# Linear attention and a gated feed-forward block: the order and the pieces of the first two batches' work

## The chip, the cores and the metric

The kernel runs on one core of a Trainium2 chip. A core has five engines with instruction queues of their own: TensorE (PE; its weight loads are listed as PEld), VectorE (DVE), ScalarE (ACT), GpSimd (POOL) and SyncE (SP). They wait for each other through semaphores. DMA transfers are issued from the queues of SP, ACT and POOL and are moved by 16 DMA engines. The metric is the time of one execution on the device, in microseconds (us); lower is better.

## The reference

For 8 batches with 8 heads each, 576 tokens and a head width of 64, linear attention is computed and then a feed-forward block with a SiLU gate, on 8 x 576 = 4608 tokens of width 512:

```python
q_s = softmax(q, axis=-1)            # over the 64 of a head
k_s = softmax(k, axis=2)             # over the 576 tokens
kv  = einsum('bhsd,bhse->bhde', k_s, v)
x   = einsum('bhsd,bhde->bhse', q_s, kv)      # heads side by side: 4608 x 512
out = (silu(x @ w_gate) * (x @ w_val)) @ w_out   # 512 -> 1536 -> 512
```

Inputs and outputs are float32. The kernel's matmuls take bfloat16 and add up in float32.

## The kernel before

**Layout.** A *group* G is four heads, two groups a batch. A partition of a raw tensor holds nine consecutive tokens (T = 9) of two heads. `load` (L72) reads q, k or v of a group as one transfer of 128 x 2 x 576 float32 values (2304 bytes a row) through SP's queue. [...]

**Attention of a group.** ACT takes the exponential of q and k (`exp_of`, L119). DVE sums exp(q) over each head, inverts the sums (`norm_sum`) and multiplies (`norm_mul`, L146), which gives `qs`. `qs` has to be transposed to `qt`: with nine TensorE transposes into two PSUM banks and two copies (`turn_pe`, `turn_out`), or by a DMA transpose (`turn_dma`, L179). TensorE contracts exp(k) with v over the tokens (`kv_first` for batch 0, `kv_one` for batch 1, `kv_both` later); a column of ones in v, or for batch 0 the matmuls of `key_sum`, gives the sum for k's softmax. The result, divided by that sum, is `kn` (`scale_first`, `scale_one`). `x_mm` multiplies `qt` by `kn`, and `x_out` casts the result into `xt`, the feed-forward block's input, transposed, with 512 features in four slices kk of 128. Slices kk 0 and 1 come from group 0, kk 2 and 3 from group 1.

**Feed-forward.** `m_unit(c0, n, m)` computes 128 of the 1536 hidden features (index m, 12 units a chunk) for n tokens: four gate matmuls (`wg`) and four value matmuls (`wv`) for each part of the tokens, SiLU on ACT (L305), product on DVE (L306) into `hr`. `o_mm(j)` contracts the 12 slices of `hr` with `w_out` for 128 tokens, `o_out` copies and `store` writes. Chunk 0 is batch 0 (576 tokens, in parts of 320 and 256), chunk 1 has 448 tokens, then chunks of 512.

**Order.** The whole program stands under a manual schedule: each engine runs its instructions in the order in which the code calls them, so the lines from L352 on are the schedule. PSUM has eight banks; `bank` (L47) hands them out, and a matmul into a reused bank waits for its last reader.

- *Start, L353 to L383.* SP loads q and k of batch 0, group 0 and then group 1. POOL, after k of group 0 has landed, issues casting transfers to bfloat16: v of group 0, v of group 1 in two pieces (L361), the slices of wg and wv in columns 0 to 255, 256 to 639, 640 to 1023 and 1024 to 1535 (L380), and w_out in four slices. [...]
- *Warm-up, L385 to L391.* `spin(n)` is n matmuls on zeros that nothing reads. Eight at the beginning, six after the first sum of exp(q), six after the first transposes (L426, L427, L435).
- *Batch 0, L428 to L452.* Sums of k, transposes, K^T V, x; then the first unit, which with `by_part` runs the whole first part of the tokens before the second.
- *Loads of batches 1 and 2, L454.* They begin when the second w_out slice has landed.
- *Batch 1, L460 to L493.* Its attention runs between o_mm(0) to o_mm(3), after chunk 0's units. Both its groups are transposed on TensorE. Batches 2 to 7 are computed inside the later chunks, with DMA transposes on SP's queue.

The softmax here doesn't subtract the row's maximum and nothing guards it: scores larger than these inputs give would overflow.

## Time and profile before

| | us |
|---|---|
| median of 12 runs (lowest, highest) | 317.52 (317.2, 318.99) |
| the profiled execution, own time | 317.69 |
| its span, first to last instruction | 315.8 |
| PE busy | 306.7 |
| DVE busy | 162.9 |
| ACT busy | 147.5 |
| first unit of chunk 0 starts | 14.51 |
| o_mm(0) starts, after chunk 0 | 39.17 |
| first unit of chunk 1 starts | 53.21 |

Times inside the span count from its start. In the lists of instructions the columns are start, duration, engine, line, operation, output and inputs, shapes, a count, and in brackets how long the engine had been idle and what ended that. "SPq", "ACTq" and "POOLq" are the queues' own time for issuing transfers. A busy PE is not PE at its peak, since matmuls overlap. In the table of windows the columns are the window, its length, the busy time and the count of instructions of PE, PEld, DVE, ACT and POOL, the granted clock of TensorE, the mean busy share of the DMA engines (over 1.00 when packets overlap) and GB/s.

### The profile page before, as it was taken

How to read it: one execution, taken by the hardware profiler on the slowest of the kernel's cores; microseconds unless marked ns; L12 is line 12 of the kernel's file. 1: busy time of each engine (PE TensorE's matmuls, PEld its weight loads, DVE VectorE, ACT ScalarE, POOL GpSimd, SP SyncE). 2: the span in 40 equal slices, each digit the busy share in tenths (PEclk: the TensorE clock that was granted, in tenths of full speed). 3: DMA queues.
4: the chain of work that ended last, by engine and by line, in shares of the span. 5: the costliest groups of instructions: out<-in, count | busy, mean ns of one | idle time of the engine just before them, and what ended most of it. 6: DMA issues, size and time to landing. Idle time of an engine off the chain costs nothing.

```text
span 315.8 us, 4885 instructions
## 1 busy us (share of the span) xinstructions
PE 306.7 (97%) x1894; PEld 151.9 (48%) x1894; DVE 162.9 (52%) x277; ACT 147.5 (47%) x218; POOL 28.0 (9%) x35
## 2 busy tenths in 40 slices
PE   6799999999999999999999999999999999999994
PEld 2477744554444444444454444544444444444443
DVE  3834486684754566455835492639354333423421
ACT  5843497634673475447454637355743113312300
POOL 2920021101100020002000200020000000000000
PEclk9999999999999999999999999999999999999999
DMA  7999999179246806490639253944310202020124
GB/s 280 184 203 206 301 394 388 54 156 369 53 88 180 336 19 127 107 398 13 141 71 362 84 112 64 323 162 104 66 40 0 66 2 66 0 69 4 31 69 102
DMA packets 39304, 45.75 MB, mean 145 GB/s; under 512 B 16368, under 2 KB 23024, under 8 KB 39280
## 3 DMA queue, kind: packets, MB, share of 16 engines
q1 hardware_dynamic: 32480, 39.99, 42.1%
q0 software_dynamic: 6640, 5.31, 10.9%
q8 instruction: 15, 0.25, 0.3%
q10 hardware_dynamic: 160, 0.13, 0.2%
q14 instruction: 9, 0.07, 0.1%
HBM read 37.75 MB, written 9.44 MB: 149 GB/s over the span
## 4 chain that ended last, share of the span: by engine, by line
PE 90%; DMA 5%; POOL 1%; ACT 1%; DVE 1%; issue 0%; SPq 0%
PE g_ps L298 29%; PE u_ps L298 29%; PE o_ps L322 27%; DMA wv<-in_moe_w_val_dram 3%; PE kv L191 3%; DMA k<-in_k_dram 2%; PE xp L267 1%; PE o_ps L342 1%; POOL wg L99 0%; POOL v L361 0%; DVE qs L152 0%; DVE rs L138 0%; PE tp L166 0%; ACT L124 0%; ACT eq L124 0%
## 5 line engine op out<-in xcount | busy, mean ns | idle before, releaser
L305 ACT ACTIVATE sg<-g_ps 128x512 bf16<-128x512 f32 (+2 forms) x120 | 65.1, 554 | 139.5 <-PE g_ps L298 132.4
L306 DVE TENSOR_TENSOR hr<-sg,u_ps 128x512 bf16<-128x512 bf16 (+2 forms) x120 | 74.5, 630 | 88.1 <-PE u_ps L298 83.6
L298 PE MATMUL u_ps<-xt,wv 128*128 128x512 bf16 (+2 forms) x480 | 111.2, 358 | 0.7 <-DMA wv<-in_moe_w_val_dram 0.6
L298 PE MATMUL g_ps<-xt,wg 128*128 128x512 bf16 (+2 forms) x480 | 111.5, 358 | 0.3 <-ACT xt L111 0.2
L322 PE MATMUL o_ps<-wo,hr 128*128 128x512 bf16 x420 | 93.6, 379 | 0.0
L298 PEld LDWEIGHTS <-wv 128*128 128x128 bf16 x480 | 46.8, 98 | 47.6 <-DMA wv<-in_moe_w_val_dram 1.4
L298 PEld LDWEIGHTS <-wg 128*128 128x128 bf16 x480 | 45.8, 98 | 45.3 <-issue 0.7
L322 PEld LDWEIGHTS <-hr 128*128 128x128 bf16 x420 | 40.9, 98 | 49.2
L113 DVE COPY o_sb<-o_ps 128x512 f32<-128x512 f32 x33 | 22.5, 680 | 39.2 <-PE o_ps L322 39.2
L127 POOL CAST vb<-v 128x1152 bf16<-128x1152 f32 x14 | 16.0, 1146 | 173.7 <-DMA v<-in_v_dram 114.6
L138 DVE TENSOR_REDUCE rs<-eq 128x18 f32<-128x1152 bf16 (+2 forms) x18 | 21.7, 1214 | 12.6 <-ACT eq L124 12.6
L152 DVE TENSOR_TENSOR qs<-eq,rr 128x1152 bf16<-128x1152 bf16 (+2 forms) x18 | 22.0, 1231 | 0.1
L124 ACT ACTIVATE eq<-q 128x1152 bf16<-128x1152 f32 (+2 forms) x18 | 18.2, 1053 | 3.6 <-DMA q<-in_q_dram 3.6
L124 ACT ACTIVATE ek<-k 128x1152 bf16<-128x1152 f32 x16 | 18.0, 1158 | 0.3 <-DMA k<-in_k_dram 0.2
L305 ACT ACT_TABLE_LOAD x12 | 15.4, 1283 | 0.2
L124 ACT ACT_TABLE_LOAD x11 | 14.1, 1283 | 0.2
L388 PE MATMUL idle<-zero 128*128 128x512 bf16 x20 | 6.4, 474 | 2.9 <-DVE rs L138 1.6
L191 PE MATMUL kv<-vb,ek 64*128 64x129 bf16 x252 | 8.7, 217 | 0.0
L191 PEld LDWEIGHTS <-ek 64*128 64x128 bf16 x252 | 7.3, 94 | 2.7 <-ACT sg L305 2.1
L275 ACT CAST xt<-xp 128x512 bf16<-128x512 f32 x12 | 6.4, 589 | 3.6 <-PE xp L267 3.6
L276 DVE CAST xt<-xp 128x512 bf16<-128x512 f32 x12 | 7.7, 682 | 0.0
L347 ACT COPY o_sb<-o_ps 128x128 f32<-128x128 f32 x2 | 0.5, 265 | 13.3 <-DMA out_dram<-o_sb 12.3
(46 smaller groups left out, 70.2 us busy)
## 6 DMA issues: line engine op xcount, KB each, us to landing
q<-in_q_dram SPq DMA_DIRECT2D x16, 576.0 KB, 5.3
k<-in_k_dram SPq DMA_DIRECT2D x16, 576.0 KB, 7.1
out_dram<-o_sb SPq DMA_DIRECT2D x70, 128.0 KB, 2.3
v<-in_v_dram SPq DMA_DIRECT2D x14, 576.0 KB, 9.0
wo<-in_moe_w_out_dram POOLq DMA_DIRECT2D x4, 384.0 KB, 16.5
wg<-in_moe_w_gate_dram POOLq DMA_DIRECT2D x2, 384.0 KB, 9.7
wv<-in_moe_w_val_dram POOLq DMA_DIRECT2D x2, 384.0 KB, 10.8
wg<-in_moe_w_gate_dram POOLq DMA_DIRECT2D x1, 512.0 KB, 13.8
```

Source lines behind the costliest of these rows:

```text
L113: eng.tensor_copy(out=out, in_=in_)
L124: nc.scalar.activation(out=e[:, t0:t1], in_=src[:, t0:t1], func=AF.Exp)
L127: nc.gpsimd.tensor_copy(out=vbs[G][:, :, 0:128].rearrange("p t (h d) -> p t h d", d=64), in_=raw["v", b, G].rearrange("p h (t d) -> p t h ...
L138: i = nc.vector.reduce_sum(out=rs[:, 2 * t0:2 * t1], in_=eq2[:, 2 * t0:2 * t1, :], axis=mybir.AxisListType.X)
L152: eng.tensor_mul(qs[:, t0:t1, :].rearrange("p t (h d) -> p (t h) d", d=64), eq2[:, 2 * t0:2 * t1, :], s["rr"][:, 2 * t0:2 * t1].to_broadca ...
L191: nc.tensor.matmul(out=kv[g][:, c:c + 129], lhsT=ek_of(b, G, g, t), rhs=vbs[G][r, t, 0:129], start=(t == 0), stop=(t == T - 1),)
L275: nc.scalar.copy(out=xt[:, 2 * G, c0:c0 + 512], in_=main[G][0])
L276: nc.vector.tensor_copy(out=xt[:, 2 * G + 1, c0:c0 + 512], in_=main[G][1])
L298: nc.tensor.matmul(out=gu[a][i][:, 0:w_], lhsT=(wg, wv)[a][:, kk, ms], rhs=xt[:, kk, c:c + w_], start=(kk == 0), stop=(kk == KT - 1),)
L305: nc.scalar.activation(out=sg[:, 0:w_], in_=g_ps[:, 0:w_], func=AF.Silu)
L306: nc.vector.tensor_mul(hr[:, m, r:r + w_], sg[:, 0:w_], u_ps[:, 0:w_])
L322: nc.tensor.matmul(out=o_ps, lhsT=hr[:, m, r0:r0 + 128], rhs=wo[:, m, :], start=(m == 0), stop=(m == MT - 1),)
```

## The change

For batch 0:

- v of both groups is loaded as one transfer each; POOL's list has one transfer less there.
- The weight slices become 0 to 127, 128 to 383, 384 to 767, 768 to 1151 and 1152 to 1535: ten transfers instead of eight.
- The warm-up has four groups before the first key sum: ten matmuls, then three each after the first piece of exp(q), after its sum, and after the reciprocal. Eight follow instead of six after the first transposes, and three more after K^T V of group 1.
- `kv_first(0)` stands ahead of `key_sum(1)`, which moves behind the first half of group 1's transposes. `kv_first(1)` comes after all of group 0's x matmuls, as before. The casts of x are dealt out to ACT and DVE in another way.
- The first unit contracts kk 0 and 1 for both parts of the tokens, then kk 2 and 3.

For batch 1:

- Group 0's q is transposed by a DMA transpose issued from ACT's queue, between the output copies of o_mm(0) and o_mm(1), instead of by TensorE and two copies on ACT.
- K^T V of group 0 moves ahead of the exponential of k of group 1; `norm_mul(1, 1)` on DVE moves ahead of the reciprocals for group 0's `kn`, whose scaling moves from DVE to ACT.
- `x_one(1, 0)` and `o_out(2)` move from behind o_mm(2) to behind group 1's transposes, K^T V and scaling, right ahead of o_mm(3).

The rest of the diff lets helpers return their instructions, drops options that are no longer used, and gives `turn_dma` the choice of a queue.

```diff
-        d = nc.gpsimd.dma_start(out=v16[0], in_=head_ap(v, 0, 0))
-        tc.add_manual_dep(d.ins, kd[0].ins.name, SYNC, reason="order of loads")
-        for t0, t1 in BANKS:
-            nc.gpsimd.dma_start(out=v16[1][:, :, 64 * t0:64 * t1], in_=head_ap(v, 0, 1, t0, t1))
+        for G in range(NG):
+            d = nc.gpsimd.dma_start(out=v16[G], in_=head_ap(v, 0, G))
+            if G == 0:
+                tc.add_manual_dep(d.ins, kd[0].ins.name, SYNC, reason="order of loads")
...
-        for c0, n in ((0, 256), (256, 384), (640, 384), (1024, 512)):
+        for c0, n in ((0, 128), (128, 256), (384, 384), (768, 384), (1152, 384)):
             w_slice(wg, moe_w_gate, c0, n)
             w_slice(wv, moe_w_val, c0, n)
...
-        spin(8)
-        spin(6, first)
+        spin(10)
+        for i in (0, 2, 4):
+            spin(3, steps[i])
         key_sum(0)
...
-        spin(6)
+        spin(8)
+        kv_first(0)
+        turn_pe(0, 1, 0)
+        scale_first(0, (nc.scalar, nc.scalar))
         key_sum(1)
-        kv_first(0)
-        scale_first(0, nc.scalar)
-        turn_pe(0, 1, 0)
         turn_pe(0, 1, 1)
         turn_out(0, 1, 0, nc.vector)
+        xp0 = x_mm(0, 0, 0), x_mm(0, 0, 1)
         turn_out(0, 1, 1, nc.vector)
-        xp0 = x_mm(0, 0, 0), x_mm(0, 0, 1)
-        kv_first(1, *BANKS[0])
-        kv_first(1, *BANKS[1])
-        x_out(0, 0, 0, xp0[0], (nc.scalar, nc.scalar))
-        x_out(0, 0, 1, xp0[1], (nc.vector, None))
-        scale_first(1, nc.vector)
-        xp1 = x_mm(0, 1, 0), x_mm(0, 1, 1)
-        x_out(0, 1, 0, xp1[0], (nc.scalar, nc.vector))
-        x_out(0, 0, 1, xp0[1], (None, nc.vector))
-        x_out(0, 1, 1, xp1[1], (nc.scalar, nc.vector))
+        kv_first(1)
+        x_out(0, 0, 0, xp0[0])
+        scale_first(1, (nc.scalar, nc.vector))
+        spin(3)
+        x_out(0, 0, 1, xp0[1])
+        x_one(0, 1)
...
-        if by_part:
-            steps.sort(key=lambda a: (a[2], a[0], a[1]))
+        if first:
+            steps.sort(key=lambda a: (a[1] // 2, a[2], a[0], a[1]))
...
-    def turn_dma(b, G):
+    def turn_dma(b, G, eng=nc.sync):
         s = st[b, G]
         qt = s["qt"] = at.tile([128, T, 128], BF16, tag="qt", name="qt")
-        nc.sync.dma_start_transpose(out=qt, in_=s["qs"].rearrange("p t c -> p (t c)"))
+        eng.dma_start_transpose(out=qt, in_=s["qs"].rearrange("p t c -> p (t c)"))
...
         norm_sum(1, 1)
         o_out(0, o_mm(0), nc.scalar)
+        turn_dma(1, 0, nc.scalar)
         o_out(1, o_mm(1), nc.scalar)
+        kv_one(1, 0)
         exp_of("k", 1, 1)
-        turn_pe(1, 0, 0)
-        turn_pe(1, 0, 1)
-        turn_out(1, 0, 0, nc.scalar)
-        turn_out(1, 0, 1, nc.scalar)
-        kv_one(1, 0)
-        scale_one(1, 0, (nc.vector, nc.vector))
         norm_mul(1, 1)
+        scale_one(1, 0, (nc.scalar, nc.scalar))
         p = o_mm(2)
-        x_one(1, 0)
-        o_out(2, p)
         turn_pe(1, 1, 0)
         turn_pe(1, 1, 1)
         turn_out(1, 1, 0, nc.scalar)
         turn_out(1, 1, 1, nc.scalar)
         kv_one(1, 1)
         scale_one(1, 1, (nc.vector, nc.vector))
+        x_one(1, 0)
+        o_out(2, p)
         p = o_mm(3)
```

## The prediction

> **What bounds the kernel now.** I read the page first. Parts 1 and 4 say that TensorE sets the time:

> ```profile
> PE 306.7 (97%) x1894; PEld 151.9 (48%) x1894; DVE 162.9 (52%) x277; ACT 147.5 (47%) x218; POOL 28.0 (9%) x35
> PE 90%; DMA 5%; POOL 1%; ACT 1%; DVE 1%; issue 0%; SPq 0%
> ```

> From about 54 us to the end the chain is matmuls without a gap, and the change leaves that work alone. So only two early stretches can move the time: the start, and the passage of batch 1 (39 to 54 us). The chain in order of time shows both:

> ```profile
> 10.93 9.56 DMA wv<-in_moe_w_val_dram
> 20.54 1.15 PE u_ps L298 x8
> ...
> 39.01 1.28 ACT L124
> 40.31 1.17 ACT eq L124
> 41.50 1.36 DVE rs L138
> 43.19 1.37 DVE qs L152
> 45.91 2.70 PE o_ps L322 x12
> ```

> The start ends on a transfer: wv of columns 256 to 639, issued at 10.93, lands at 20.49, and unit 2 waits for it. From there each unit of chunk 0 takes 1.95 us (0.98 gate, 0.98 value) until 39.0. The second stretch ends on batch 1's softmax. The timeline there shows what comes late and the operation that the change borrows:

> ```profile
> 14.51 0.75 PE L298 MATMUL g_ps<-xt,wg 128*128 128x320 bf16 x4
> 15.88 0.72 PE L298 MATMUL u_ps<-xt,wv 128*128 128x320 bf16 x4 [0.62 <-DMA wv<-in_moe_w_val_dram]
> 43.13 1.16 ACT L124 ACTIVATE eq<-q 128x1152 bf16<-128x1152 f32 x1 [0.61 <-DMA q<-in_q_dram]
> 44.47 1.34 DVE L138 TENSOR_REDUCE rs<-eq 128x18 f32<-128x1152 bf16 x1
> 46.90 1.64 DVE L152 TENSOR_TENSOR qs<-eq,rr 128x1152 bf16<-128x1152 bf16 x1
> 50.14 2.27 PEld L322 LDWEIGHTS <-hr 128*128 128x128 bf16 x12
> 52.84 0.44 PE L220 MATMUL xp<-qt,kn 64*64 64x320 bf16 x8
> 53.97 0.54 PE L298 MATMUL g_ps<-xt,wg 128*128 128x448 bf16 x2 [0.20 <-ACT xt L111]
> 62.00 5.12 SPq L182 DMA_TRANSPOSE qt<-qs  x2
> ```

> ACT waits for q of batch 1, group 1 (landed 43.11). o_mm(3) starts at 50.14, chunk 1's first unit at 53.21. Last, the windows: the DMA engines are full all through the passage.

> ```profile
> 39.00:44.40 5.40, 5.40 (x27) 2.36 (x25) 3.65 (x5) 4.77 (x5) 1.14 (x1) 1.00 1.06 398
> 44.40:53.20 8.80, 8.71 (x95) 4.54 (x94) 6.30 (x15) 6.88 (x11) 1.15 (x1) 1.00 1.05 390
> ```

> [...] the first eight warm-up matmuls stand 0.43 us apart, those after 6.33 us 0.22 us apart.

> **The change, part by part.**

> *Weight slices.* Every slice is 512 packets whatever its width, 32 for each of 16 engines. Counted in the trace's packet records, one engine spends 46 ns on a packet of 512 bytes written (256 columns), 61 ns on 768 and 80 ns on 1024, about 12 ns plus 0.066 ns a byte. Then 384 columns cost 1.96 us, 256 cost 1.47, 512 cost 2.56; 128 columns (256 bytes, in no transfer of the kind here) I put at 29 ns, 0.93 us. Bounds: 23 ns by bytes alone, 46 ns as for 512 bytes. V of group 1 as one transfer: 16 packets of 88 ns, 1.41 us, against 16 of 54 and 16 of 46, 1.60: 0.19 saved.

> Before, wg and wv up to column 639 take 2 x (1.47 + 1.96) = 6.86 us; after, up to column 767, 2 x (0.93 + 1.47 + 1.96) = 8.72. The value slice that unit 3 needs lands 8.72 - 6.86 - 0.19 = 1.67 us later than the one unit 2 waited for, but one unit later is 1.95: chunk 0 gains 0.28 and ends at 38.7. (wv of columns 128 to 383 lands at 18.25, which gives unit 3's value half the same 22.2.) At the low price the gain is 0.7, at the high one a loss of 0.8. All slices together are 16.56 against 15.90: everything queued behind them, batch 1's loads too, lands 0.66 - 0.19 = 0.47 later (0.1 to 1.6).

> *K^T V order, unit 0 by groups, casts.* kv_first(0) no longer stands behind key_sum(1), but V lands at 10.96 and before it ran at 11.09: nothing gained. key_sum(1) now stands ahead of the second transposes; its reciprocal on DVE puts the qt copies and the group 1 scale 0.2 later, so unit 0 starts at about 14.55 and, with weights there at 14.6, ends near 16.6 instead of 17.3. The wait for wv hides all of this; without that cover it would be worth 0.5 to 0.7.

> *Warm-up.* 19 + 8 + 3 matmuls instead of 14 + 6: they fill idle PE time (4.69 to 6.33, 9.0 to 10.75, and 0.65 at 13.5 while the scale runs to 14.15). Cost nothing under that cover, 10 x 0.22 = 2.2 us without it. The clock was already full in this execution, so no gain.

> *Batch 1's passage.* Removed from PE: nine transposes (0.6) and from ACT two copies (1.2). Added: one DMA transpose on ACT's queue; on SP its issue takes 1.33 and it lands 3.3 after its start, with no load beside it. Behind it on ACT stand o_out(1), the exponential of k, the two kn scales. norm_mul(1, 1) moves ahead of the group 0 reciprocals. PE: o_mm(0), o_mm(1), kv, o_mm(2) follow from 38.7 to about 47.1. Then TensorE waits: q lands 43.11 + 0.47 = 43.58; exponential to 44.75; sum to 46.15; reciprocal to 46.45; product (1.36 to 1.64) to 48.0; transposes to 48.6. The reciprocals of K^T V end at 48.4, the two ACT scales (0.37 each) at 49.15, the two qt copies (1.2) at 50.35. o_mm(3) takes the PSUM bank that the last copy frees: 50.4 at the earliest, against 50.14. So the 0.28 gained and the 0.6 removed both end in a wait for q.

> x_one(1, 0) now stands ahead of o_mm(3) and needs the transposed qt. qs(1, 0) is ready at 44.3; undisturbed it lands at 47.6, hidden. But SP's queue holds six loads of batches 1 and 2 until 55.5, and an engine's share of one load is 16 packets of 93 ns, 1.49 us. The transpose has 72 descriptors for an engine (1152 packets counted), [...] two turns lost, up to 2.98, give 50.6. x_one's 0.4 then puts o_mm(3) at 51.05: **+0.9 us** against 50.14, and the x casts behind the two exponentials on ACT move as much. From there PE is gapless as before.

> Sum against the profiled execution: 317.69 (its span 315.8 and 1.89 around it) + 0.9 = 318.6. That execution lies 0.17 above the median of the runs, so I predict **318.4** from 317.52. No change can be told from less than about 0.2%, 0.63 us.

> **Rivals.**
> 1. *The transpose is hidden* (one turn or none lost, landed by 49.3). For it: 1.7 us of slack at 3.3. Against: full DMA engines. o_mm(3) then starts at 50.4: +0.25, 317.8.
> 2. *The transpose goes to the end of the loads*: [...] it lands at 55 to 57. [...] 322 to 326. [...]
> 3. *Faster*: if qs(1, 1) is ready by 47.2, PE never waits, and the removed 0.6 and the 0.28 count: chunk 1 starts near 52.2, 316.5. It decides at q landed by 42.8 us, 0.3 earlier than now; against it, the loads get later by my count.
> 4. *256-byte packets at 46 ns*: batch 1's q lands 1.6 later, and the passage follows: +1.5 to 2, 319.3.

> **How the numbers follow.** Forecast 0.35, rival 1 0.25, rival 2 0.2, rival 3 0.12, rival 4 0.08. The forecast's own range is 318.0 to 319.2. The range for 8 in 10 runs from 316.9 to 322.5: it leaves out most of rival 3 and the longer half of rival 2. Faster by over 0.2% is rival 3: 0.12. Within 0.2%: rival 1 and the low edge of the forecast, 0.3. Slower: 0.58.

> **What would show it.** Right: wv waits gone at 15.88, one near 18 or 22; chunk 0 ending near 38.7; q at 43.6; a PE gap before the batch 1 transposes near 48; x_one(1, 0) released by the DMA transpose at 50 to 51; chunk 1's first unit near 54.1. Wrong: x_one released by ACT (rival 1), a transpose landing of 10 us (rival 2), no gap at 47 (rival 3).

## The result, and the profile after

| | before | after |
|---|---|---|
| median of the runs (lowest, highest), us | 317.48 (317.03, 318.99) | 327.72 (326.85, 328.36) |
| ratio (95% interval) | | 1.0318 (1.0305 to 1.0331) |
| the profiled execution, own time | 317.69 | 326.91 |
| its span | 315.8 | 325.0 |
| o_mm(0) starts | 39.17 | 38.14 |
| first unit of chunk 1 starts | 53.21 | 62.42 |

The changed kernel is 3.2% slower. I had forecast 318.4 with a range of 316.9 to 322.5. The result lies above the range and above the 322 to 326 of rival 2, whose outcome is what happened: the transpose lands at the end of the loads, at 56.49. TensorE's clock falls as well, to half from 51.41 to 61.65.

The page of the kernel after: busy times, the granted clock in 40 slices, the chain that ended last.

```profile
PE 310.9 (96%) x1895; PEld 153.4 (47%) x1895; DVE 162.2 (50%) x275; ACT 147.1 (45%) x218; POOL 29.9 (9%) x36
PEclk9999996799999999999999999999999999999999
PE 81%; DMA 15%; POOL 1%; SPq 1%; ACT 1%; issue 0%; DVE 0%
```

PE is busy for 4.2 us more than before although it has nine transposes less. Part of that is the ten more warm-up matmuls (9.8 us of them in place of 6.4). The other part belongs to the loss: the clock line has a dip in slices 7 and 8 (49 to 65 us), and slow matmuls are long matmuls (95.8 us of output matmuls in place of 93.6). DMA's share of the chain went from 5% to 15%. The chain in order of time, up to batch 1, names the piece:

```profile
10.05 6.93 DMA wv<-in_moe_w_val_dram
17.27 15.41 DMA wo<-in_moe_w_out_dram
34.21 8.35 DMA q<-in_q_dram
42.58 0.97 ACT eq L124
43.55 12.94 DMA qt<-qs
57.23 4.89 PE o_ps L323 x12
```

The DMA transpose takes 12.94 us from its issue to its landing, the moment at which its semaphore lets the waiting engine go on (landing at 56.49, x_one(1, 0) at 56.53). In the kernel before, the twelve transposes of the later batches, batch 2's with hardly another packet beside them, took 3.3:

```profile
DMA to landing us min/median/max: 3.2/3.3/3.3
```

What the chain shows ahead of the transpose is doubtful. It names the exponential of group 1's q, and behind that the loads and the weights. But the issue at 43.55 follows the product qs of group 0, which the transpose reads, by 0.03 us (42.16 + 1.36 = 43.52), and it follows that product by 0.03 or 0.04 in five of the six other runs that issue it from ACT's queue. So the transpose was most likely released by DVE, behind chunk 0's units, and not by q, and part of the 15% isn't DMA's. The timeline of the kernel after (columns as before):

```profile
12.88 0.68 PE L411 MATMUL kv<-v,ek 64*128 64x128 bf16 x18 [0.26 <-DMA v<-in_v_dram]
...
14.61 0.45 PE L299 MATMUL g_ps<-xt,wg 128*128 128x320 bf16 x2
...
42.16 1.36 DVE L153 TENSOR_TENSOR qs<-eq,rr 128x1152 bf16<-128x1152 bf16 x1
42.58 1.16 ACT L124 ACTIVATE eq<-q 128x1152 bf16<-128x1152 f32 x1 [1.09 <-DMA q<-in_q_dram]
43.55 1.37 ACTq L183 DMA_TRANSPOSE qt<-qs  x1
45.46 1.36 DVE L153 TENSOR_TENSOR qs<-eq,rr 128x1152 bf16<-128x1152 bf16 x1
46.88 0.68 PE L167 MATMUL tp<-ident,qs 128*128 128x128 bf16 x9
47.88 0.70 PE L192 MATMUL kv<-vb,ek 64*128 64x129 bf16 x18 [0.33 <-POOL vb L128]
56.53 0.69 PE L221 MATMUL xp<-qt,kn 64*64 64x320 bf16 x8 [7.96 <-DMA qt<-qs]
57.16 4.96 PE L323 MATMUL o_ps<-wo,hr 128*128 128x512 bf16 x12
62.42 0.55 PE L299 MATMUL g_ps<-xt,wg 128*128 128x448 bf16 x2
```

No unit waits for weights at the start any more. TensorE is idle for 7.96 us ahead of x_one(1, 0), until the transpose has landed, and the twelve matmuls of o_mm(3) then take 4.96 us in place of 2.76. In the kernel before:

```profile
50.15 2.76 PE L322 MATMUL o_ps<-wo,hr 128*128 128x512 bf16 x12
```

The windows show both (the last three figures of a row are the granted clock, the busy share of the DMA engines and GB/s):

```profile
39.00:44.40 5.40, 5.40 (x41) 2.60 (x40) 3.72 (x5) 4.11 (x5) 1.14 (x1) 1.00 1.05 392
44.40:53.20 8.80, 3.78 (x39) 2.10 (x37) 3.44 (x9) 3.34 (x6) 2.21 (x1) 0.90 1.08 358
47.00:60.00 13.00, 4.72 (x42) 2.32 (x41) 2.36 (x7) 4.43 (x8) 3.12 (x3) 0.67 0.79 259
```

From 47 to 60 us PE works for 4.72 of 13 us, at a mean clock of 0.67; in the kernel before the same window has 12.80 us of PE at 1.00:

```profile
47.00:60.00 13.00, 12.80 (x97) 6.27 (x96) 7.28 (x14) 10.34 (x16) 2.62 (x3) 1.00 0.77 279
```

The sum closes: o_mm(3) starts 57.16 - 50.15 = 7.01 us later and takes 2.20 longer, 9.21 together; the profiled executions differ by 326.91 - 317.69 = 9.22. After chunk 1's first unit PE has no gap in either kernel.

### The profile page after: what moved, and what is told of

Read it like the earlier page. It is cut to its first block, busy times and chain, and to the rows that moved or that the text cites. A ratio compares the mean times of both kernels' runs of the same rounds, so it can differ in the third digit from the quotient of the medians.

```text
span 325.0 us, 4887 instructions
## 1 busy us (share of the span) xinstructions
PE 310.9 (96%) x1895; PEld 153.4 (47%) x1895; DVE 162.2 (50%) x275; ACT 147.1 (45%) x218; POOL 29.9 (9%) x36
## 4 chain that ended last, share of the span: by engine, by line
PE 81%; DMA 15%; POOL 1%; SPq 1%; ACT 1%; issue 0%; DVE 0%
PE o_ps L323 26%; PE g_ps L299 25%; PE u_ps L299 25%; DMA wo<-in_moe_w_out_dram 5%; DMA qt<-qs 4%; DMA q<-in_q_dram 3%; DMA wv<-in_moe_w_val_dram 2%; PE kv L192 2%; DMA k<-in_k_dram 1%; PE xp L268 1%; PE o_ps L343 1%; SPq L77 1%; POOL v L360 0%; POOL wg L99 0%; PE xp L221 0%
## 5 line engine op out<-in xcount | busy, mean ns | idle before, releaser
L323 PE MATMUL o_ps<-wo,hr 128*128 128x512 bf16 x420 | 95.8, 385 | 0.0
L113 DVE COPY o_sb<-o_ps 128x512 f32<-128x512 f32 x33 | 22.5, 680 | 39.2 <-PE o_ps L323 39.2
L128 POOL CAST vb<-v 128x1152 bf16<-128x1152 f32 x14 | 17.1, 1222 | 180.7 <-DMA v<-in_v_dram 180.4
L138 DVE TENSOR_REDUCE rs<-eq 128x18 f32<-128x1152 bf16 (+2 forms) x18 | 21.7, 1215 | 12.7 <-ACT eq L124 12.7
L124 ACT ACTIVATE eq<-q 128x1152 bf16<-128x1152 f32 (+2 forms) x18 | 18.1, 1050 | 3.8 <-DMA q<-in_q_dram 3.7
L124 ACT ACTIVATE ek<-k 128x1152 bf16<-128x1152 f32 x16 | 17.9, 1158 | 0.3 <-DMA k<-in_k_dram 0.2
L389 PE MATMUL idle<-zero 128*128 128x512 bf16 x30 | 9.8, 494 | 1.2 <-DVE sel L368 1.2
L113 DVE CAST xt<-xp 128x128 bf16<-128x128 f32 (+2 forms) x14 | 5.1, 379 | 11.8 <-PE xp L221 11.8
L111 ACT CAST xt<-xp 128x128 bf16<-128x128 f32 (+2 forms) x14 | 4.6, 351 | 11.9 <-PE xp L221 11.9
L221 PE MATMUL xp<-qt,kn 64*64 64x320 bf16 (+1 forms) x32 | 2.0, 330 | 8.0 <-DMA qt<-qs 8.0
```

The source lines that it names most:

```text
L111: nc.scalar.copy(out=out, in_=in_)
L113: eng.tensor_copy(out=out, in_=in_)
L124: nc.scalar.activation(out=e[:, t0:t1], in_=src[:, t0:t1], func=AF.Exp) for t0, t1 in pieces
L128: nc.gpsimd.tensor_copy(out=vbs[G][:, :, 0:128].rearrange("p t (h d) -> p t h d", d=64), in_=raw["v", b, G].rearrange("p h (t d) -> p t h ...
L138: nc.vector.reduce_sum(out=rs[:, 2 * t0:2 * t1], in_=eq2[:, 2 * t0:2 * t1, :], axis=mybir.AxisListType.X)
L323: nc.tensor.matmul(out=o_ps, lhsT=hr[:, m, r0:r0 + 128], rhs=wo[:, m, :], start=(m == 0), stop=(m == MT - 1),)
```

## The experiments

Diffs are against the kernel after unless it is said otherwise. "The passage" is the code from o_mm(0) to o_mm(3).

### Which half of the change costs the time

**The start of the kernel after with the passage of the kernel before.**

```diff
         o_out(0, o_mm(0), nc.scalar)
-        turn_dma(1, 0, nc.scalar)
         o_out(1, o_mm(1), nc.scalar)
-        kv_one(1, 0)
         exp_of("k", 1, 1)
-        norm_mul(1, 1)
-        scale_one(1, 0, (nc.scalar, nc.scalar))
+        turn_pe(1, 0, 0)
+        turn_pe(1, 0, 1)
+        turn_out(1, 0, 0, nc.scalar)
+        turn_out(1, 0, 1, nc.scalar)
+        kv_one(1, 0)
+        scale_one(1, 0, (nc.vector, nc.vector))
+        norm_mul(1, 1)
         p = o_mm(2)
+        x_one(1, 0)
+        o_out(2, p)
...
-        x_one(1, 0)
-        o_out(2, p)
         p = o_mm(3)
```

> The start of the changed kernel, with batch 1's passage as before. Theory (all of the loss is in the passage, the start gains 1.0 us): chunk 0 ends near 38.1 instead of 39.2, and at least half of that survives the passage, which now waits for q of group 1: 316.5 to 317.0. Rival (the start's gain ends in a wait for q, landed at about 42.6): 317.3 to 317.6, with a gap of TensorE near 44 or 48. Rival (the start itself costs): over 318.

Measured: 317.92 us, 1.0021 (1.0007 to 1.0034), between the ranges of my two rivals; the start doesn't gain the 0.5 to 1.0 us of my theory, it costs a little. In its profile o_mm(0) starts at 38.75 and chunk 1 at 52.92, 0.3 before the kernel before, but the median doesn't show it.

**The start of the kernel before with the passage of the kernel after.** Against the kernel before, the same lines the other way round (and `turn_dma` with the choice of a queue):

```diff
...
         o_out(0, o_mm(0), nc.scalar)
+        turn_dma(1, 0, nc.scalar)
         o_out(1, o_mm(1), nc.scalar)
+        kv_one(1, 0)
         exp_of("k", 1, 1)
-        turn_pe(1, 0, 0)
...
+        x_one(1, 0)
+        o_out(2, p)
         p = o_mm(3)
```

> The start of the kernel before, with the changed kernel's passage of batch 1. Theory: the DMA transpose on ACT's queue lands 12 to 13 us after its issue, TensorE stands idle for about 8 us near 49 to 57, and the next output matmuls run at half clock: 327.0 to 328.5. Rival (the earlier start is what makes the transpose collide with the loads): below 322.

Measured: 327.33 us, 1.0310 (1.0297 to 1.0324), as the theory said. Its timeline has the same wait:

```profile
57.44 0.69 PE L220 MATMUL xp<-qt,kn 64*64 64x320 bf16 x8 [7.53 <-DMA qt<-qs]
```

The passage alone gives the loss, to within the intervals (1.0310 and 1.0318).

### What of it is the clock

**36 matmuls on zeros in the wait.**

```diff
         scale_one(1, 1, (nc.vector, nc.vector))
+        spin(36)
         x_one(1, 0)
```

> The changed kernel with 36 matmuls on zeros (7.8 us at full clock) ahead of the x matmuls of batch 1, group 0, where TensorE stood idle. Theory: the idle time itself stays, but the 12 output matmuls after it run 0.22 us apart instead of 0.43: 2.2 to 2.5 us less than the changed kernel, 325.2 to 325.6. Rival (the clock costs nothing that is on the path): 327.7 as the changed kernel.

Measured: 325.23 us, 1.0246 (1.0233 to 1.0259), clock 1.00 throughout. In this kernel the transpose lands as late, 12.9 us after its issue at 44.30, and o_mm(3) runs at full speed:

```profile
57.28 0.44 PE L221 MATMUL xp<-qt,kn 64*64 64x320 bf16 x8
...
57.66 2.76 PE L323 MATMUL o_ps<-wo,hr 128*128 128x512 bf16 x12
```

So 36 matmuls on zeros in the wait give back 2.5 us of the median (327.72 to 325.23; 2.20 is what o_mm(3) lost in the profile). The rest, some 7.7 us, is the wait, 7.01 in the profile, and the 0.2% that the start costs.

### Is it the meeting with the loads

**The loads of batch 2 only after the transpose has landed.**

```diff
-        load_batch(2)
...
-        turn_dma(1, 0, nc.scalar)
+        tr = [turn_dma(1, 0, nc.scalar)]
+        load_batch(2, tr[0])
```

> The changed kernel, but the six loads of batch 2 are issued only when the DMA transpose has landed. Theory (the transpose shares the DMA engines one descriptor for one with the loads): beside the rest of batch 1's loads alone it lands within 4 to 7 us of its issue, the 8 us gap of TensorE shrinks to under 2, and the time is 316.5 to 319, with the loads of batch 2 later. Rival (a transpose on ACT's queue is slow by itself): still 12 to 13 us, 328 or more. Rival (the new order on ACT and DVE makes the gap, not the transpose): the landing is early, the gap stays near 8 us, over 325.

Measured: 321.36 us, 1.0115 (1.0084 to 1.0145). The timeline of this kernel:

```profile
44.12 1.53 ACTq L183 DMA_TRANSPOSE qt<-qs  x1
49.14 0.44 PE L221 MATMUL xp<-qt,kn 64*64 64x320 bf16 x8
49.52 2.76 PE L323 MATMUL o_ps<-wo,hr 128*128 128x512 bf16 x12
52.24 1.16 ACT L124 ACTIVATE eq<-q 128x1152 bf16<-128x1152 f32 x1 [2.03 <-DMA q<-in_q_dram]
55.54 0.54 PE L299 MATMUL g_ps<-xt,wg 128*128 128x448 bf16 x2 [2.40 <-ACT xt L111]
```

With only the tail of batch 1's loads beside it, the transpose lands at 48.27, 4.15 us after its issue, and x_one(1, 0) waits for nothing. That half of the expectation came true: it is the loads. The time missed it. In the profile the loads are late next: ACT waits 2.03 us for q of batch 2 with x_one(1, 1)'s casts queued behind, and TensorE waits 2.40 us for the casts. This execution took 319.39, the shortest of the four; what the other three (320.58 to 322.44) add, no profile shows.

**Only k and v of batch 2 held back.**

```diff
-        load_batch(2)
+        load("q", q, 2, 0)
+        load("q", q, 2, 1)
...
-        turn_dma(1, 0, nc.scalar)
+        tr = turn_dma(1, 0, nc.scalar)
+        load("k", k, 2, 0, after=tr)
+        load("k", k, 2, 1)
+        load("v", v, 2, 0)
+        load("v", v, 2, 1)
```

> The kernel after, with k and v of batch 2 loaded only when the DMA transpose of batch 1 has landed; q of batch 2 is loaded as before. Theory, the loss is the meeting of the transpose with the six loads of batch 2: with two of them in its way instead of six, its descriptors find free engines once the second has ended near 48.5, and it lands at 49.5 to 50.5 in place of 56.5. The clock stays full, o_mm(3) starts near 50.5, q of batch 2 is there in time for ACT (which had waited for it when all six were held back), k lands near 53.5: 317.8 to 319.0. Rival, the held back loads are what is late next: a wait for k or v of batch 2 stops TensorE in chunk 1 and the time is 319.5 to 322.

Measured: 321.61 us, 1.0128 (1.0113 to 1.0142). This missed, and not by its rival: k and v came in time, but the transpose landed only at 52.12, 7.8 us after its issue, though the last load packet in its way ended at 49.45 by the records. TensorE had been idle for 2.82 us, and the clock fell (0.87 in the mean from 47 to 60 us):

```profile
52.16 0.44 PE L221 MATMUL xp<-qt,kn 64*64 64x320 bf16 x8 [2.82 <-DMA qt<-qs]
...
52.54 4.44 PE L323 MATMUL o_ps<-wo,hr 128*128 128x512 bf16 x12
```

The packet records show where the time went: 20 packets of the transpose begin between 47.41 and 48.89 and all end between 49.79 and 49.83 (more on this in the last section); the other packets after that end at 51.30.

### How the transpose gets through

The trace has a record of each packet with its bytes, its beginning and its end, but not its engine. I take each packet for one descriptor. The transpose has 1152 of 256 bytes, which is 72 an engine if the 16 have equal shares, and a load has 256 of 2304 bytes. In the kernel after, the packets that end in each microsecond, of all 16 engines, are:

```
us           47   48   49   50   51   52   53   54   55
256 bytes    44   57  153  155  167  158  166  177   75
2304 bytes  156   64  139  148  157  145  160   90   27
```

From 49 to 54 us that is 799 packets of the transpose to 749 of the loads. Equal counts alone could also come of equal turns of several packets. The times at which packets begin tell the two apart. Of all pairs of transpose packets that begin between 49.1 and 54 us, those 100 to 110 ns apart are 2.5 times as frequent as by chance and those 200 to 210 ns apart 2.2 times, while those 50 to 60 ns apart have only 0.2 of that. About 100 ns is one load packet (93 ns) and one transpose packet (18 ns), a little overlapped; several transpose packets in a row would stand some 20 ns apart. And 80 to 90 ns after a load packet has begun, a transpose packet begins 2.1 times as often as by chance. By this, one packet of the transpose went for one of the loads while both were there. That this holds on each single engine is an inference, and what makes the two alternate isn't shown.

The first packet starts at 47.62, 4.07 us after the issue (1.29 where all of batch 2's loads were held back, 2.58 where k and v were), the last ends at 55.73, and the landing is at 56.49. Against the run with all of batch 2's loads held back, where first to last takes 1.91, the start is 2.8 us later and first to last 6.2 longer; of that 6.2, some 0.8, by my estimate, is a standstill at 48.3 to 49.0: from 48.5 to 49.0 only 8 packets end, where 124 did from 47.5 to 48.0 (see the last section).

**Five of the nine tiles by DMA.**

```diff
-        eng.dma_start_transpose(out=qt, in_=s["qs"].rearrange("p t c -> p (t c)"))
+        h = BANKS[0][1] if eng is nc.scalar else T
+        eng.dma_start_transpose(out=qt[:, 0:h, :], in_=s["qs"][:, 0:h, :].rearrange("p t c -> p (t c)"))
...
         o_out(1, o_mm(1), nc.scalar)
+        turn_pe(1, 0, 1)
+        turn_out(1, 0, 1, nc.scalar)
```

> The kernel after, but only the first five of the nine 128-column tiles of group 0's qs go through the DMA transpose (640 descriptors, 40 an engine, in place of 72); the other four are transposed on TensorE and copied by ACT, after o_mm(1). Theory, one descriptor for one: the transpose's descriptors pass at the same pace as in the kernel after, about 113 ns apiece and engine, so first to last takes 40 x 0.113 = 4.5 us in place of 8.1, and it lands near 52.9 in place of 56.5. TensorE stands idle from about 49.1 to 53.0, and the time is 323.5 to 324.5 with the half clock, 321.5 to 322.2 if the shorter idle time no longer brings it. Rival, [...] order of arrival: the landing moves by one load's share at most, 1.5 us: 55 us and 326 to 327.

Measured: 325.44 us, 1.0237 (1.0213 to 1.0261), between the theory's range and the rival's. In its profile chunk 0 ends 1.1 us later than in the kernel after (o_mm(0) at 39.24), and with it comes the issue, at 44.65:

```profile
54.72 0.70 PE L222 MATMUL xp<-qt,kn 64*64 64x320 bf16 x8 [5.18 <-DMA qt<-qs]
```

Counted from the issue, the first packet starts after 4.17 us and the landing comes after 9.93, where one for one asked for 9.35 and the rival for about 11.4. The counts agree with one for one: between the beginning of the first and the end of the last packet stand 640 of the transpose and 629 of loads, over 4.95 us. So do the beginnings: from 49.6 to 53 us, transpose packets 100 to 110 ns apart are 2.9 times as frequent as by chance, those 50 to 60 ns apart 0.3 times.

**Loads of batch 2 in halves.**

```diff
-        for h in ((0, 1), (1, 2)) if by_head else ((0, 2),):
-            last = nc.sync.dma_start(out=t_[:, h[0]:h[1], :], in_=head_ap(src, b, G, h))
+        for t0, t1 in ((0, 5), (5, T)) if by_head else ((0, T),):
+            ap = bass.AP(tensor=src.tensor, offset=src[b, 4 * G].offset + 64 * t0, ap=[[T * 64, 128], [2 * HSTR, 2], [1, 64 * (t1 - t0)]])
+            last = nc.sync.dma_start(out=t_[:, :, 64 * t0:64 * t1], in_=ap)
...
-            load(w, s, b, G, after=after)
+            load(w, s, b, G, after=after, by_head=(b == 2))
```

> The kernel after, but each load of batch 2 goes as two transfers, tokens 0 to 4 and 5 to 8 of every partition: descriptors of 1280 and 1024 bytes, 54 and 46 ns each on an engine, in place of 2304 bytes and 93 ns. Theory, one descriptor for one: a pair of a load's and a transpose's descriptor then takes about 50 + 20 = 70 ns, so the 72 of an engine take 5.0 us from the first to the last in place of 8.1. If the first one comes at 47.6 us as in the kernel after, the landing is near 53.4, [...] the time is 324 to 325; if the first one also comes earlier because it waits for a number of descriptors, the landing is near 52 and the time 322 to 323.5. Rival, turns whose length is a count of bytes or a share of a transfer: landing at 55.5 or later and 326.5 to 328.

Measured: 325.18 us, 1.0241 (1.0218 to 1.0264). Time and landing (10.1 us after the issue) are near what I expected, but not for my reason: between first and last packet stand 1152 of the transpose and only 463 of loads. SP issued the loads of v at 47.8 to 51.2, in place of 42.6 and 44.1, and from 50 to 51 us only 46 load packets ended beside 276 of the transpose: the loads ran short, so this run can't confirm the one for one. What the run does show is that the first packet again starts 4.08 us after the issue: that delay, 4.07 us in the kernel after, didn't shrink with the descriptors of the loads.

**The transpose on SP's queue, behind the loads.**

```diff
-        turn_dma(1, 0, nc.scalar)
+        turn_dma(1, 0)
```

> The kernel after, with the transpose issued on SP's queue, behind the loads of batch 2 and the first output, in place of ACT's. Theory: a queue runs in order, so it follows the last load, which without it ends near 54.5, and takes about 1.6 us of packets by itself; it lands at 56.5 to 57.5 and the time is 327 to 328.5, so that a row of its own on ACT's queue gained at most 1 us. Rival, it is served between the loads here too: landing at 53 or earlier, 323 to 325.

Measured: 328.16 us, 1.0332 (1.0319 to 1.0345), as expected. The transpose was issued at 48.66, behind the loads; its first packet starts at 54.24 and it lands at 57.75, 0.25 later than expected. Beside 1.0318 for the kernel after (1.0305 to 1.0331), the way past the loads on ACT's queue gained at most a little against waiting for them: 0.4 us in the median, which the intervals don't tell apart.

### The order, and the start

**The order of the kernel after, with TensorE's transposes.**

```diff
-        turn_dma(1, 0, nc.scalar)
         o_out(1, o_mm(1), nc.scalar)
+        turn_pe(1, 0, 0)
+        turn_pe(1, 0, 1)
+        turn_out(1, 0, 0, nc.scalar)
+        turn_out(1, 0, 1, nc.scalar)
```

> The kernel after, with its start and its order in batch 1's passage, but group 0's q is transposed on TensorE (nine transposes after o_mm(1), two copies on ACT) in place of the DMA transpose. Theory, the loss is the late transpose alone: no wait for a DMA ahead of x_one(1, 0); q of group 1 lands near 42.6 to 43.1, its product ends near 47, ACT's queue (the exponential of k, two kn scales, four qt copies) ends near 49.3, o_mm(3) starts at 49.3 to 50, chunk 1's first unit at 52.5 to 53: 316.8 to 317.6. Rival, the order itself costs something as well (x_one(1, 0) and o_out(2) late, casts late): o_mm(3) after 50.4 and over 318.

Measured: 318.26 us, 1.0024 (1.0014 to 1.0034). This is the rival's range (over 318), but not by its cause: o_mm(3) starts at 50.13, where the rival asked for more than 50.4, and beside 1.0021 for the start alone, the order in the passage costs nothing that can be told, and gains nothing. All but 0.2% of the loss is the DMA transpose.

**That 0.2%**, in three runs. Against the kernel before, its weight slices alone:

```diff
-        for c0, n in ((0, 256), (256, 384), (640, 384), (1024, 512)):
+        for c0, n in ((0, 128), (128, 256), (384, 384), (768, 384), (1152, 384)):
```

> The kernel before with only the weight slices of the kernel after (128, 256, 384, 384, 384 columns). Theory, the start of the kernel after gains nothing in the median because it puts v of group 1 in one transfer, on whose last engine x of group 1 now waits; with before's two pieces of v and the new slices no unit waits for weights, o_mm(0) starts at 38.5 to 38.8 in place of 39.17, and a third to a half of that reaches the end: 317.0 to 317.3. Rival, whatever the start gains ends in the wait for q of batch 1, group 1, whose landing the weights set: 317.4 to 317.7.

The start of the kernel after without these slices, and the passage of the kernel before (the lines of the first experiment, and in the start):

```diff
-        for c0, n in ((0, 128), (128, 256), (384, 384), (768, 384), (1152, 384)):
+        for c0, n in ((0, 256), (256, 384), (640, 384), (1024, 512)):
```

> The start of the kernel after (v in whole transfers, order of batch 0, warm-up) with the weight slices of the kernel before (256, 384, 384, 512 columns), and the passage of the kernel before. Theory, the 0.2% that the start alone cost comes with the new slices, since the kernel before with only these showed most of it (1.0014): without them the time is that of the kernel before, 317.3 to 317.7, and the value half of unit 2 waits for its slice again. Rival, v in whole transfers and the order cost it: 317.8 to 318.2, with K^T V of group 1 released by v at 13.0 us or later.

The kernel with the order and TensorE's transposes, with q of group 1 loaded third:

```diff
             order = [(w, s, G) for G in range(NG) for w, s in qkv]
+            order.insert(2, order.pop(3))
```

> The kernel with the start and the order of the kernel after and all transposes of batch 1 on TensorE (measured at 1.0024), with q of batch 1, group 1 loaded third instead of fourth, ahead of v of group 0. Theory, what the start gains ends in the wait for that q (1.82 us of idle ACT in that kernel's trace): q lands 1.5 us earlier, near 42.0, the exponential follows the one of k without a wait, and chunk 1's first unit starts at 52.4 to 52.9 in place of 53.18: 317.3 to 317.8. Rival, the passage hangs on DVE (sum, product, sum, product without a gap from 40.8) or on v of group 0, which now lands later: 318.0 to 318.5.

| | ratio (95% interval) | own time of the profile | o_mm(0) | eq(1, 1) | chunk 1 |
|---|---|---|---|---|---|
| before | | 317.69 | 39.17 | 43.13 | 53.21 |
| only the slices | 1.0014 (1.0004 to 1.0024) | 317.50 | 38.84 | 43.05 | 52.89 |
| the start without the slices | 1.0019 (1.0005 to 1.0034) | 317.94 | 39.22 | 42.98 | 53.27 |
| the start | 1.0021 (1.0007 to 1.0034) | 317.48 | 38.75 | 43.15 | 52.92 |
| the start and the order | 1.0024 (1.0014 to 1.0034) | 318.10 | 38.45 | 43.62 | 53.18 |
| the same, q earlier | 1.0019 (1.0009 to 1.0029) | 318.83 | 39.61 | 42.87 | 54.03 |

The medians are 318.06 with only the slices, 318.30 without them, and 318.25 with q earlier. Here the theories failed; only the rival of the last run, that the passage hangs on DVE or on v, has its range met. Two kernels with disjoint parts of the start's edits both measure 0.14 to 0.19%, and both parts together no more. Loading q earlier took away ACT's wait for it (eq(1, 1) follows ek(1, 0) at once), but the median stayed: v of group 0 came later, its cast took 2.34 us beside DVE's product, and kv_one(1, 0) waited 0.32 for it. Chunk 0 also ended 1.2 us later in that profile than without the change. A profile shows one execution, and the start of the first unit moves from 14.19 to 15.71 us between the ten profiled kernels with the start of the kernel after; in most of them K^T V of group 1 waits for v, now one transfer. Why the medians lie above the kernel before while several profiles lie below it is left open.

## Why the prediction was wrong

- **The step that failed: "two turns lost, up to 2.98, give 50.6."** To the 47.6 of an undisturbed transpose I had added two of a load's shares of an engine, 2 x 1.49 us. That the loads would cost it just two was my estimate; no trace had shown it. While load descriptors were there, the records show one descriptor of the loads for each of the transpose (799 to 749; 640 to 629 with five tiles; a repeat of about 100 ns). So 72 descriptors of an engine cost some 72 times one of each: 8.1 us from the first to the last in place of 1.9. (The step's own sum is 0.05 high: 50.58 and 0.4 give 51.0.) Nor could the kernel before have told it: where its last w_out slice meets the load of q, from 35 to 36.75 us, the slice's packets that begin in a quarter of a microsecond fall from 40 to 3 and those of the loads rise from 11 to 38, but there the slice is running out, so it doesn't show two queues that are both full.
- **The start of the transpose.** I had counted nothing between the issue and the first packet beyond the undisturbed case. Beside the loads of batch 2 it took 4.07 to 4.17 us in five runs, 2.58 with k and v held back, 1.29 with all six held back. Why is open; a count of descriptors in front doesn't fit, since it took 4.08 with the loads in halves too.
- **Rival 2 had the right end, a little short.** Its landing at 55 to 57 holds (56.49). That doesn't mean that the transpose was served after the loads: 799 of its packets end among 749 of theirs. Its time of 322 to 326 fell short: the clock alone was worth 2.5 us (327.72 to 325.23 with the matmuls on zeros), and the median lies 0.8 above the profiled execution, which had an early start. I gave it 0.2 and ended the range at 322.5, inside it.
- **o_mm(3) at 51.05** became 57.16, and the +0.9 became +9.2. My phrase "from there PE is gapless" held.
- **Weight slices.** No transfer of 256-byte packets had been seen; 636 of them end from 12 to 13 us on 16 engines, 25 ns each, where I took 29 from bounds of 23 and 46. The slice of columns 384 to 767 of wv lands at 21.02, where I had 22.2, and rival 4 is out.
- **Chunk 0 gains 0.28.** In the profile of the kernel after it gains 1.03. Over the ten profiled kernels with that start o_mm(0) starts at 38.14 to 39.61, 38.79 in the mean; the two profiled kernels with the start of before have 39.17 and 39.39. So 0.4 to 0.5 in the mean: the term was about right, and the profiled execution of the kernel after had an early start.
- **Batch 1's loads 0.47 later**: q(1, 1) landed at 42.55 in the kernel after, not at 43.58; in the other kernels with its slices and its order of loads eq(1, 1) starts between 43.05 and 44.09, where it starts at 43.13 in the kernel before: the sign is right in most, and the size too large.
- **The passage up to the transposes of group 1** went as worked out, a us sooner: the product qs(1, 1) at 45.46, then the transposes. The gap of PE ahead of them, some 0.9 us by my times, is only 0.08, so TensorE hardly waited for q there, as rival 3 had it; the transpose hides what that was worth. kv_one(1, 1) waited 0.33 for the cast of v, which took 2.21 us instead of 1.15 while DVE's product ran; I hadn't seen that.
- **Warm-up and K^T V order costing nothing**: not told apart; with the slices they are within the 0.2% above.

## What to carry to other kernels

Before a transfer is put on a path that an engine waits for, count its descriptors on each DMA engine and the time of one descriptor of whatever else is queued there: here one descriptor of the loads went for each of the transpose (749 to 799), and first to last took 8.1 us in place of 1.9. A DMA transpose that is hidden in a quiet stretch (3.3 us) is no price for the same transpose among loads (12.9 us). Holding the loads back moved part of the wait, because they were needed soon as well. And a chain view names the releaser that it infers: check it against the moment at which the data was ready.
